# Decode order in the last network, splits of the last expert, and the end of the retention stage rearranged together

## The chip, the cores and the metric

One core of one Trainium2 chip runs the program. The time is device microseconds (us) of one execution of the whole program; lower is better. The engines are TensorE (PE, matrix products), VectorE (DVE), ScalarE (ACT), GpSimd (POOL) and SyncE (SP, which only issues DMAs here). Each works off its own instructions in the order in which the program wrote them, and waits at an instruction until what it needs is there.

## What is computed

Three networks in a row: a retention layer, a mixture of eight experts with one expert per token and limited places, and a network with a maximum of three products.

```python
def _attn_ref(q, k, v):                      # (4, 8, 576, 64) each
    scores = scale * np.matmul(q, k.transpose(0, 1, 3, 2))
    Dmat = np.where(rel >= 0, gamma[:, None, None] ** rel[None, :, :], 0.0)
    ret = scores * Dmat[None, :, :, :]
    return np.matmul(ret, v).astype(np.float32)

def _moe_ref(x, w_gate, w1, w2, capacity):   # x (2304, 512), E = 8, F = 1024
    logits = x @ w_gate
    expert_idx = np.argmax(logits, axis=1)
    ...                                      # probs: softmax; gate_w: its value at expert_idx
    for i in range(N):
        e = expert_idx[i]
        if counts[e] < capacity:
            disp[e, counts[e]] = x[i]; pos[i] = counts[e]; counts[e] += 1; keep[i] = True
    h = np.maximum(np.einsum('ecd,edf->ecf', disp, w1), 0.0)
    y = np.einsum('ecf,efd->ecd', h, w2)
    ...                                      # out[i] = gate_w[i] * y[expert_idx[i], pos[i]] where keep

def _moe2_ref(x, w1, w2, w3, w_out):         # 512 -> 768 -> 512
    h = np.maximum(np.maximum(x @ w1, x @ w2), x @ w3)
    return (h @ w_out).astype(np.float32)
```

Products are made in a precision close to float32: each operand is held as a high and a low part, and a product is three matmuls (high by high, high by low, low by high; L1095 to L1097, and their likes at L1135 and L1291).

## The kernel before

**Retention and gating (0 to 132 us).** The 2304 tokens go in 18 chunks of at most 128 rows (5 per batch element; the fifth has 64). A loop over `t` makes the scores of the next chunk (`scores`, `cut`), its outputs (`outputs`), and for earlier chunks the transposes (`transposes`, L487), the choice of expert (`gate1`, `position`, `gate2`), and the send of the scaled row into the DRAM table `xd`. Chunks 0 to 13 are gated in three groups (`group_choose`, `group_place`, `group_weigh`, `group_send`); a group is placed at the chunk two behind its last, and two of its rows of chunks are sent per chunk from then on. The last chunks (`NPATCH` = 3: 15, 16, 17) go to expert 0 another way: their rows don't come back out of `xd`. Expert 0's input is collected in the four PSUM tiles `fx`: `patch(u, c)` (L612) multiplies the rows of chunk u (`part`, high and low) by a selection matrix, and `turn(c)` (L620) adds, transposed, the rows that three indirect DMAs of POOL (`load_x(0)`, L170, r0 to r2) gathered from `xd`. `finish_part` makes the low part of `part` on DVE (L550) and sends the scaled `xg`. `seats` (L636) makes the tables of places. `first_x` splits `fx` into the high and low part that expert 0 reads.

**Experts (132 to 369 us).** For each expert, `mm1` has eight steps f (an output tile of 128 of the 1024 hidden columns, written as h by ACT, L1111, and its low part by DVE), and `mm2` four. Weights come as raw tiles of 512 KB (three buffers), and `next_split` makes the high part on ACT (L140) and the low part on DVE (L145) and then issues the next load on SP. A split stands behind each odd f and each step of `mm2`, and for expert 0 behind f = 2, 4 and 6 as well.

**Decode.** The last network's weights arrive as 64-bit numbers and are turned into float32 on the chip, in 24 pieces of 512 columns (`NDEC`): two ACT operations (`dec_act`, L1005 and L1006), four on DVE (`decode_top` L1020, L1023; `decode` L1031, L1034), two on POOL (L1037, L1038), and a write of POOL's queue to the DRAM table `wdec`. `NSOON` of them, 12, are decoded in the expert stage, at the steps that the table `per` names, and are loaded and split like other weights later. `per` has a tuple for each expert, of its 12 steps (eight f, then four of `mm2`).

**The pair (368.6 to 470.0 us).** The last network has six tiles of 384 tokens (i) and six hidden tiles (f). `up(i, f)` makes three products of 36 matmuls in all, into three of the six PSUM tiles; ACT copies the first (L1265, into m, or into a free part of y), DVE takes two maxima (L1266, L1267), ACT writes h (L1268) and DVE its low part (L1269). The first 12 steps, i = 0 and 1 in turn for each f, are the pair. In it the remaining 12 pieces are decoded. A late piece lies in a part of y, with two places in turn: `dec_act(n + 1)` waits until piece n - 1 has been written out of it. `take_unit` (L1063 on ACT, L1064 on DVE) makes the unit w out of a finished piece. How many pieces follow each step is the list `LATER`:

```python
LATER = [1, 1, 1, 2, 1, 1, 2, 1, 2]
        ...
                for _ in range(LATER[step] if step < len(LATER) else 0):
                    if n > NSOON:
                        take_unit(n - 1)
                    decode_top(n)
                    done[n] = decode(n)
                    n += 1
                    dec_act(n)
```

After the pair, `down` (L1291) and `up` for the other tiles run to 702.2 us.

## Time and profile before

| | us |
|---|---|
| median of three runs | 703.53 (703.26 to 704.21) |
| the profiled execution | 704.04 |
| its span | 702.2 |
| PE busy | 658.9 (94%) |
| DVE busy | 353.3 (50%) |
| ACT busy | 258.1 (37%) |
| POOL busy | 196.7 (28%) |

The span begins with the first instruction and ends with the last one; 1.84 us of the profiled execution's time lie outside it. All times of rows are counted from the start of the span. Busy shares are means over four stages that have different limits, so they are only a first look; which engine waits in a stage, and for whom, is read from the waits of PE, from its windows and from the chain of waits. The "granted clock" of a window is TensorE's clock as a share of 2.4 GHz; 0.50 is the lower of its two levels, 1.2 GHz.

### The profile page before, as it was taken

To read this page: it belongs to the slowest core of one execution; us is meant where nothing else is said; L and a number is where in the kernel's file an instruction comes from. 1 tells how busy PE (TensorE), PEld (TensorE's weight loads), DVE (VectorE), ACT (ScalarE), POOL (GpSimd) and SP (SyncE) were. 2 spreads that over 40 slices of the span, in tenths; PEclk is the share of its full clock that TensorE was granted. 3 is DMA by queue.
4 is the path that set the end of the run, shared out by engine and by line. 5 is a ranking of instruction groups with operands and counts; after the bars stand their busy time and mean duration, and the time that the engine had idled before them with its cause. 6 is when DMAs were issued, how large, how long until landed. Compare 5 with 4: busy or idle time off the path is not lost.

```text
span 702.2 us, 11814 instructions
## 1 busy us (share of the span) xinstructions
PE 658.9 (94%) x4631; PEld 623.2 (89%) x4631; DVE 353.3 (50%) x727; ACT 258.1 (37%) x478; POOL 196.7 (28%) x180
## 2 busy tenths in 40 slices
PE   8998997989999999999999957789999999999995
PEld 6887876989999999999999957788999999998994
DVE  3487686565757777776465646560032131131120
ACT  3344343255555556465454333331112121111111
POOL 1001122136555652677401354431100100101001
PEclk9999999599999999999999989789999999999998
DMA  8999932265786878767432333301100100000001
GB/s 279 326 265 291 356 96 61 94 177 188 221 196 203 237 218 245 212 218 210 134 135 68 117 102 116 109 30 46 46 0 1 46 1 15 31 1 31 15 1 47
DMA packets 42930, 91.01 MB, mean 130 GB/s; under 512 B 16778, under 2 KB 18702, under 8 KB 42872
## 3 DMA queue, kind: packets, MB, share of 16 engines
q1 hardware_dynamic: 25848, 64.73, 30.2%
q0 software_dynamic: 14624, 21.36, 9.7%
q10 hardware_dynamic: 2400, 4.14, 1.6%
q8 instruction: 38, 0.62, 0.4%
q14 instruction: 20, 0.16, 0.1%
HBM read 73.68 MB, written 16.47 MB: 128 GB/s over the span
## 4 chain that ended last, share of the span: by engine, by line
PE 73%; DMA 9%; ACT 5%; DVE 5%; issue 4%; POOL 3%; ACTq 1%; SPq 0%; POOLq 0%; DVEq 0%
PE b L1135 16%; PE u L1095 8%; PE u L1096 8%; PE u L1097 8%; PE a L1095 5%; PE a L1096 5%; PE a L1097 5%; PE d L1292 3%; PE d L1293 3%; PE d L1291 3%; DMA wdec<-y 3%; DMA kv<-in_kv_dram 2%; PE xps L487 2%; PE tp L968 1%; DMA xr<-xd,who 1%
## 5 line engine op out<-in xcount | busy, mean ns | idle before, releaser
L1095 PE MATMUL u<-ys,w 128*128 128x384 f32 x414 | 141.7, 342 | 18.9 <-ACT y L1265 8.2
L1096 PE MATMUL u<-ys,w 128*128 128x384 f32 x414 | 140.8, 340 | 0.0
L1097 PE MATMUL u<-ys,w 128*128 128x384 f32 x414 | 140.7, 340 | 0.0
L1135 PE MATMUL b<-h,w 128*128 128x336 f32 (+7 forms) x768 | 118.4, 308 | 3.3 <-ACT h L1111 2.7
L145 DVE TENSOR_TENSOR w<-raw,w 128x1024 fp32r<-128x1024 f32 x70 | 93.5, 1335 | 52.8 <-ACT w L140 45.3
L1135 PEld LDWEIGHTS b<-h,w 128*128 128x128 f32 x768 | 109.8, 190 | 4.4 <-ACT h L1111 3.3
L1095 PEld LDWEIGHTS u<-ys,w 128*128 128x128 f32 x414 | 79.8, 193 | 20.4 <-ACT y L1265 8.5
L1266 DVE TENSOR_TENSOR m<-u,m 128x384 f32<-128x384 f32 x30 | 16.7, 557 | 131.5 <-PE u L1097 115.9
L140 ACT ACTIVATE w<-raw 128x1024 fp32r<-128x1024 f32 x70 | 73.9, 1056 | 18.5 <-DMA raw<-in_weights_dram 17.0
L1096 PEld LDWEIGHTS u<-ys,w 128*128 128x128 f32 x414 | 79.9, 193 | 0.2
L1097 PEld LDWEIGHTS u<-ys,w 128*128 128x128 f32 x414 | 79.6, 192 | 0.2 <-DVE w L1064 0.2
L1095 PE MATMUL a<-xt,w 128*128 128x336 f32 (+7 forms) x256 | 78.5, 307 | 0.0
L1096 PE MATMUL a<-xt,w 128*128 128x336 f32 (+7 forms) x256 | 78.3, 306 | 0.0
L1097 PE MATMUL a<-xt,w 128*128 128x336 f32 (+7 forms) x256 | 78.2, 305 | 0.0
L1297 POOL DMA_INDIRECT out_dram<-o,perm_sb x18 | 17.4, 968 | 213.4 <-ACT o L1295 209.3
L1268 ACT ACTIVATE h<-m 128x384 fp32r<-128x384 f32 x28 | 14.7, 526 | 106.2 <-DVE m L1267 106.2
L1095 PEld LDWEIGHTS a<-xt,w 128*128 128x128 f32 x256 | 48.9, 191 | 0.9 <-issue 0.5
L1096 PEld LDWEIGHTS a<-xt,w 128*128 128x128 f32 x256 | 49.0, 191 | 0.0
L1097 PEld LDWEIGHTS a<-xt,w 128*128 128x128 f32 x256 | 48.9, 191 | 0.0
L170 POOL DMA_INDIRECT xr<-xd,who x24 | 37.3, 1554 | 35.3 <-DVE order_w L1156 21.9
L183 POOL DMA_INDIRECT who_d<-tok,slots_i x20 | 21.1, 1054 | 91.8 <-DMA who_d<-tok,slots_i 49.5
L1111 ACT ACTIVATE h<-a 128x336 fp32r<-128x336 f32 (+7 forms) x64 | 26.6, 423 | 33.6 <-PE a L1097 30.7
(216 smaller groups left out, 1025.8 us busy)
## 6 DMA issues: line engine op xcount, KB each, us to landing
raw<-in_weights_dram SPq DMA_DIRECT2D x64, 512.0 KB
kv<-in_kv_dram SPq DMA_DIRECT2D x16, 512.0 KB
qk<-in_qk_dram SPq DMA_DIRECT2D x15, 512.0 KB
y<-in_weights_dram SPq DMA_DIRECT2D x12, 512.0 KB
d<-in_weights_dram POOLq DMA_DIRECT2D x10, 512.0 KB
xd<-xg ACTq DMA_DIRECT2D x14, 256.0 KB
wdec<-mag POOLq DMA_DIRECT2D x12, 256.0 KB
raw<-wdec SPq DMA_DIRECT2D x6, 512.0 KB
```

Of the source, the lines that this page charges most:

```text
L140: act.activation(out=t[:, 0], in_=raws[w], func=AF.Copy)
L145: engine.tensor_tensor(out=t[:, 1], in0=raws.pop(w), in1=t[:, 0].bitcast(F32), op=ALU.subtract)
L170: pool.indirect_dma_start(out=xr[:n, r, :], out_offset=None, in_=xd[:, :], in_offset=bass.IndirectOffsetOnAxis(ap=who[:n, r, e : e + 1] if ...
L183: pool.indirect_dma_start(out=who_d[:, :], out_offset=bass.IndirectOffsetOnAxis(ap=slots_i[:L, t : t + 1], axis=0), in_=tok[:L, t : t + 1] ...
L1095: pe.matmul(ps, lhsT=wh, rhs=xh, start=first, stop=False)
L1096: pe.matmul(ps, lhsT=wh, rhs=xl, start=False, stop=False)
L1097: pe.matmul(ps, lhsT=wl, rhs=xh, start=False, stop=last)
L1111: act.activation(out=h[:, 0, :wide], in_=ps, func=AF.Relu)
L1135: pe.matmul(ps, lhsT=w[:, a, f * P : (f + 1) * P], rhs=hs[f][:, b, :wide], start=(i == 0), stop=(i == len(todo) - 1),)
L1291: pe.matmul(ps, lhsT=hh, rhs=wh, start=(f == 0), stop=False)
L1292: pe.matmul(ps, lhsT=hh, rhs=wl, start=False, stop=False)
L1293: pe.matmul(ps, lhsT=hl, rhs=wh, start=False, stop=(f == NFF - 1))
```

## The change

Four parts, all at once.

1. **Pair.** `NSOON` goes from 12 to 16, so 8 pieces stay for the pair, one for each of its first eight steps. The four more early ones: one in expert 5 (at place 5), two in expert 6 (5 and 8), one in expert 7 (2). The work on a piece is no longer written behind the step but inside `up`, by three callbacks: a finished piece's high part goes ahead of the maxima, the decode's four DVE operations stand between the maxima and the low part of h, and the finished piece's low part and the next `dec_act` follow behind it. 72 instead of 70 units are split; the last `next_split` stands behind the last `mm2`.
2. **Splits.** The extra splits at f = 2, 4, 6 go from expert 0 to expert 7.
3. **Groups.** The sends of groups 0 and 1 start one chunk later, and their `group_place` is moved into the middle of `outputs`; the last group's stays, now ahead of `cut(t + 1)`.
4. **End of retention.** `finish_part(16)` is done in the loop: ACT scales `xg` first, and POOL subtracts for the low part. `position(17)` no longer stands behind turns; then come `patch(16, c)`, the turns of r0 and r1 for all c, `seats(16)`, and in `first_x` for each c the turn of r2 with `patch(17, c)`; `seats(17)` and the count come after.

```diff
 NDEC = 2 * NFF * NPIECE
-NSOON = NDEC // 2
-LATER = [1, 1, 1, 2, 1, 1, 2, 1, 2]
+NSOON = 2 * NDEC // 3
...
                         )
+                    dve.tensor_tensor(out=acc[:L], in0=acc[:L], in1=oh[:L], op=ALU.add)
                     rows(t, xg, xps, g2)
...
                 part, xg, g2 = patch_t[t][0][0], xg_t.pop(t), g_t.pop(t)
-                dve.scalar_tensor_tensor(
-                    out=part[:L, 1], in0=xg[:L], scalar=g2[:L], in1=part[:L, 0].bitcast(F32),
-                    op0=ALU.mult, op1=ALU.subtract,
-                )
-                act.activation(out=xg[:L], in_=xg[:L], func=AF.Copy, scale=g2[:L])
+                if t == NCHUNK - 2:
+                    act.activation(out=xg[:L], in_=xg[:L], func=AF.Copy, scale=g2[:L])
+                    pool.tensor_tensor(out=part[:L, 1], in0=xg[:L], in1=part[:L, 0].bitcast(F32), op=ALU.subtract)
+                else:
+                    dve.scalar_tensor_tensor(
+                        out=part[:L, 1], in0=xg[:L], scalar=g2[:L], in1=part[:L, 0].bitcast(F32),
+                        op0=ALU.mult, op1=ALU.subtract,
+                    )
+                    act.activation(out=xg[:L], in_=xg[:L], func=AF.Copy, scale=g2[:L])
                 sp.dma_start(out=xd[1 + t0 : 1 + t0 + L, :], in_=xg[:L])
...
-            def turn(c):
-                for r, n in slots_of(0):
-                    pe.matmul(
-                        fx[c][:, r * RP : r * RP + n], lhsT=xr_t[0][:n, r, c * P : (c + 1) * P],
-                        rhs=ident[:n, :n], start=False, stop=False, skip_group_check=True,
-                    )
+            def turn(c, r, n):
+                pe.matmul(
+                    fx[c][:, r * RP : r * RP + n], lhsT=xr_t[0][:n, r, c * P : (c + 1) * P],
+                    rhs=ident[:n, :n], start=False, stop=False, skip_group_check=True,
+                )
             def first_x():
                 xt = xpool.tile([P, 2, NC, TILE2], F32R, tag="xt", name="xt0")[:, :, :, : WIDTH[0]]
                 for c in range(NC):
+                    turn(c, *slots_of(0)[-1])
                     patch(NCHUNK - 1, c)
                     split_x(xt, c, fx[c])
                 xt_t[0] = xt
...
                 for j in range(len(g)):
-                    sends.setdefault(g[-1] + 2 + j // 2, []).append((i, j))
+                    sends.setdefault(g[-1] + 2 + (i < len(GROUPS) - 1) + j // 2, []).append((i, j))
             for t in range(NCHUNK):
...
                     gate1(t - 1)
-                if t + 1 in sc_t:
+                early = t in placed and placed[t] == len(GROUPS) - 1
+                if t + 1 in sc_t and not early:
                     cut(t + 1)
...
                     update(t + 1)
-
-                if t in placed:
+                if early:
                     group_place(placed[t])
+                    cut(t + 1)
                 def place():
+                    if t in placed and not early:
+                        group_place(placed[t])
                     if ok(t - 1) and t - 1 not in GROUP_OF:
...
                     pick(t - 1)
-                    if t < NCHUNK - 1:
-                        finish_part(t - 1)
+                    finish_part(t - 1)
                 if ok(t - 1) and t - 1 not in GROUP_OF:
...
             seats(first)
-            seats(last - 1)
-            turn(0)
-            turn(1)
             position(last)
-            finish_part(last - 1)
             gate2(last)
             gate3(last)
-            for c in range(2, NC):
-                turn(c)
             for u in range(first + 1, last):
...
                     patch(u, c)
+            for r, n in slots_of(0)[:-1]:
+                for c in range(NC):
+                    turn(c, r, n)
+            seats(last - 1)
+            first_x()
             seats(last)
...
             dve.tensor_copy(out=cnt, in_=cnt_p)
-            first_x()
...
-        def take_unit(n):
+        def into_unit(n):
...
                 units[w] = home.tile([P, 2, 1024], F32R, tag="w", name=f"w{w}")
-            t = units[w]
-            act.activation(out=halves(t[:, 0, cols]), in_=mag, func=AF.Copy)
-            dve.tensor_tensor(
-                out=halves(t[:, 1, cols]), in0=mag, in1=halves(t[:, 0, cols]).bitcast(F32), op=ALU.subtract
-            )
+            hi, lo = (halves(units[w][:, k, cols]) for k in range(2))
+            act.activation(out=hi, in_=mag, func=AF.Copy)
+            return lambda: dve.tensor_tensor(out=lo, in0=mag, in1=hi.bitcast(F32), op=ALU.subtract)
         LAST = F // P + NC
-        per = [(8,), (2, 8), (2, 8), (2, 8), (2, 8), (2, 8), (2,), ()]
+        per = [(8,), (2, 8), (2, 8), (2, 8), (2, 8), (2, 5, 8), (2, 5, 8), (2,)]
         slots = [e * LAST + k for e in range(E) for k in per[e]]
...
                     units.pop(8 * e + f // 2)
-                if f % 2 or (e == 0 and f in (2, 4, 6)):
+                if f % 2 or (e == E - 1 and f in (2, 4, 6)):
                     if (e, f) != (0, 1):
...
         m2p = m2["pool"]
+        next_split()
         for c in range(NC):
...
-        def up(i, f, m, h):
+        def up(i, f, m, h, beside=(lambda: None,) * 3):
             wa, wb = units[8 * E + 2 * f], units[8 * E + 2 * f + 1]
...
             act.activation(out=m, in_=pss[0], func=AF.Copy)
+            beside[0]()
             dve.tensor_tensor(out=m, in0=pss[1], in1=m, op=ALU.max)
...
             act.activation(out=hi, in_=m, func=AF.Copy)
+            beside[1]()
             dve.tensor_tensor(out=lo, in0=m, in1=hi.bitcast(F32), op=ALU.subtract)
+            beside[2]()
             h2_t[i, f] = h
...
         early_h = m2p.tile([P, 2, NC, TILE2], F32R, tag="ys", name="early_h")
-        step, n = 0, NSOON
-        dec_act(n)
+
+        after = {}
+
+        def before_max(n):
+            if n in done:
+                after[n] = into_unit(n)
+
+        def behind_max(n):
+            if n < NDEC:
+                decode_top(n)
+                done[n] = decode(n)
+
+        def behind_h(n):
+            if n - 1 in after:
+                after.pop(n - 1)()
+            if n + 1 < NDEC:
+                dec_act(n + 1)
+
+        dec_act(NSOON)
+        n = NSOON
         for f in range(NFF):
             for i in range(2):
-                up(i, f, new_m(i, f), early_h[:, :, 2 * f + i] if f < 2 else new_h(i, f))
-                for _ in range(LATER[step] if step < len(LATER) else 0):
-                    if n > NSOON:
-                        take_unit(n - 1)
-                    decode_top(n)
-                    done[n] = decode(n)
-                    n += 1
-                    dec_act(n)
-                if step == len(LATER):
-                    take_unit(n - 1)
-                    assert n == NDEC
+                up(
+                    i, f, new_m(i, f), early_h[:, :, 2 * f + i] if f < 2 else new_h(i, f),
+                    (lambda: before_max(n - 1), lambda: behind_max(n), lambda: behind_h(n)),
+                )
+                n += 1
                 if (i, f) == (0, NFF - 1):
...
                         ysplit_part(2, c)
-                step += 1
         down(0)
```

How the order of the engines changes is shown at three places.

PE at the end of the retention stage, before (`fx_1654` to `fx_1657` are the four tiles c, `xr_1517` the gathered rows with r0 and r1 as x2, `po` is position(17)):

```order
L620 MATMUL fx_1655<-cst,xr_1517 128x118 x2
L620 MATMUL fx_1655<-cst,xr_1517 128x100
L493 LDWEIGHTS tri
L493 MATMUL po_1701<-oh_1682,tri 64x8
L499 LDWEIGHTS ones
L499 MATMUL po_1701<-acc,ones 64x8
L620 MATMUL fx_1656<-cst,xr_1517 128x118 x2
L620 MATMUL fx_1656<-cst,xr_1517 128x100
L620 MATMUL fx_1657<-cst,xr_1517 128x118 x2
L620 MATMUL fx_1657<-cst,xr_1517 128x100
L612 MATMUL fx_1654<-sel_1643,part_0_1644 128x336 x2
L612 MATMUL fx_1655<-sel_1643,part_0_1644 128x336 x2
```

After (tiles `fx_1657` to `fx_1660`):

```order
L492 LDWEIGHTS tri
L492 MATMUL po_1695<-oh_1685,tri 64x8
L498 LDWEIGHTS ones
L498 MATMUL po_1695<-acc,ones 64x8
L617 MATMUL fx_1657<-sel_1643,part_0_1644 128x336 x2
L617 MATMUL fx_1658<-sel_1643,part_0_1644 128x336 x2
L617 MATMUL fx_1659<-sel_1643,part_0_1644 128x336 x2
L617 MATMUL fx_1660<-sel_1643,part_0_1644 128x336 x2
L624 MATMUL fx_1657<-cst,xr_1517 128x118
L624 MATMUL fx_1658<-cst,xr_1517 128x118
L624 MATMUL fx_1659<-cst,xr_1517 128x118
L624 MATMUL fx_1660<-cst,xr_1517 128x118
```

Position(17) and the patches of chunk 16 moved ahead of all turns; r1 (four more rows of the same kind), three rows of `who_p` and then r2 in turn with the patches of chunk 17 follow.

DVE in the pair, step i = 1, f = 1, before (`y<-u` the maxima, `early_h` the low part of h, `w` a finished piece's low part, `y<-y` the decode):

```order
L1266 TENSOR_TENSOR y<-u_1_1_4746,y 128x2x192
L1267 TENSOR_TENSOR y<-u_1_2_4747,y 128x2x192
L1269 TENSOR_TENSOR early_h<-y,early_h 128x384
L1064 TENSOR_TENSOR w_4789<-y,w_4789 128x512
L1020 TENSOR_SCALAR y<-y 128x2x256
L1023 SCALAR_TENSOR_TENSOR y<-y 128x2x256
L1031 SCALAR_TENSOR_TENSOR y<-y 128x2x256
L1034 TENSOR_SCALAR y<-y 128x2x256
L1064 TENSOR_TENSOR w_4789<-y,w_4789 128x512
L1020 TENSOR_SCALAR y<-y 128x2x256
L1023 SCALAR_TENSOR_TENSOR y<-y 128x2x256
L1031 SCALAR_TENSOR_TENSOR y<-y 128x2x256
```

After:

```order
L1271 TENSOR_TENSOR y<-u_1_1_4808,y 128x2x192
L1272 TENSOR_TENSOR y<-u_1_2_4809,y 128x2x192
L1025 TENSOR_SCALAR y<-y 128x2x256
L1028 SCALAR_TENSOR_TENSOR y<-y 128x2x256
L1036 SCALAR_TENSOR_TENSOR y<-y 128x2x256
L1039 TENSOR_SCALAR y<-y 128x2x256
L1275 TENSOR_TENSOR early_h<-y,early_h 128x384
L1069 TENSOR_TENSOR w_4847<-y,w_4847 128x512
```

One decode in place of two, and it moved ahead of the low part of h; the second decode of this step is gone.

ACT in expert 7's first products, before (`h` the output of a step f, `w<-raw` a split):

```order
L1111 ACTIVATE h_2_4321<-a_2_4308 128x272
L1111 ACTIVATE h_3_4338<-a_3_4325 128x272
L140 ACTIVATE w_4341<-raw_4236 128x1024
L1111 ACTIVATE h_4_4359<-a_4_4346 128x272
L1111 ACTIVATE h_5_4376<-a_5_4363 128x272
L140 ACTIVATE w_4379<-raw_4268 128x1024
L1111 ACTIVATE h_6_4397<-a_6_4384 128x272
L1111 ACTIVATE h_7_4414<-a_7_4401 128x272
L140 ACTIVATE w_4417<-raw_4306 128x1024
```

After:

```order
L1114 ACTIVATE h_2_4353<-a_2_4340 128x272
L139 ACTIVATE w_4356<-raw_4262 128x1024
L1114 ACTIVATE h_3_4380<-a_3_4367 128x272
L139 ACTIVATE w_4383<-raw_4294 128x1024
L1114 ACTIVATE h_4_4401<-a_4_4388 128x272
L139 ACTIVATE w_4404<-raw_4332 128x1024
L1114 ACTIVATE h_5_4423<-a_5_4410 128x272
L139 ACTIVATE w_4426<-raw_4359 128x1024
L1114 ACTIVATE h_6_4444<-a_6_4431 128x272
L139 ACTIVATE w_4447<-raw_4386 128x1024
```

A split moved in behind f = 2, 4 and 6; in expert 0 these three splits went, and its steps look there as expert 7's did here.

## Rows read from the trace of the kernel before

**Rows 1.** Waits of PE over the span: total us, times, longest.

```profile
PE u L1095 <- ACT y L1265: 8.2, 1, 8.2
PE u L1095 <- ACT m L1265: 7.2, 1, 7.2
PE u L1095 <- ACT w L1063: 3.6, 1, 3.6
```

**Rows 2.** Windows of PE: length, busy (instructions), granted clock, DMA share, GB/s.

```profile
368.60:470.00 101.40, 82.51 (x434) 0.88 0.30 94
...
500.84:538.30 37.46, 37.46 (x217) 1.00 0.02 8
121.50:136.90 15.40, 15.40 (x60) 0.50 0.33 111
132.30:136.90 4.60, 4.60 (x17) 0.50 0.50 175
```

**Rows 3.** Chain of waits in the pair: start, us, what.

```profile
384.84 5.32 DMA wdec<-y
...
421.76 4.04 DMA wdec<-y
```

**Rows 4.** Groups of instructions in the pair, by shape: busy, mean ns, idle before.

```profile
L1037 POOL TENSOR_TENSOR y<-y 128x512 f32<-128x512 f32 x11 | 14.2, 1295 | 75.2 <-DVE y L1034 38.8 <-issue 26.8 <-ACT y L1265 5.5
...
L1031 DVE SCALAR_TENSOR_TENSOR y<-y 128x512 f32<-128x512 f32 x12 | 8.3, 692 | 0.4
...
L1005 ACT ACTIVATE y<-y 128x512 f32<-128x512 f32 x12 | 8.0, 669 | 40.2 <-DMA wdec<-y 31.9 <-DMA y<-in_weights_dram 3.9 <-DVE y L1034 3.1
L1064 DVE TENSOR_TENSOR w<-y,w 128x512 fp32r<-128x512 f32 x11 | 7.6, 692 | 11.1 <-ACT w L1063 11.1
...
L1034 DVE TENSOR_SCALAR y<-y 128x512 int32<-128x512 int32 x12 | 5.1, 427 | 0.4
...
L1266 DVE TENSOR_TENSOR m<-u,m 128x384 f32<-128x384 f32 x5 | 2.8, 558 | 15.6 <-ACT m L1265 15.6
```

**Rows 5.** Chain of waits in the retention stage.

```profile
59.52 12.43 DMA kv<-in_kv_dram
```

**Rows 6.** Timelines of ACT, then of PE, at the end of expert 0's first product.

```profile
151.62 1.06 ACT L140 ACTIVATE w<-raw 128x1024 fp32r<-128x1024 f32 x1 [5.43 <-DMA raw<-in_weights_dram]
...
149.22 2.00 PE L1135 MATMUL b<-h,w 128*128 128x336 f32 x12
153.07 0.58 PE L1135 MATMUL b<-h,w 128*128 128x336 f32 x2 [1.84 <-ACT h L1111]
154.51 3.11 PE L1135 MATMUL b<-h,w 128*128 128x336 f32 x10 [0.86 <-ACT h L1111]
```

**Rows 7.** Timelines of ACT in experts 5 and 7, then of DVE in expert 7.

```profile
298.58 1.06 ACT L140 ACTIVATE w<-raw 128x1024 fp32r<-128x1024 f32 x1 [2.56 <-DMA raw<-in_weights_dram]
...
350.74 0.40 ACT L1111 ACTIVATE h<-a 128x272 fp32r<-128x272 f32 x1 [1.11 <-PE a L1097]
...
352.24 0.40 ACT L1111 ACTIVATE h<-a 128x272 fp32r<-128x272 f32 x1 [0.15 <-PE a L1097]
...
352.12 1.23 DVE L145 TENSOR_TENSOR w<-raw,w 128x1024 fp32r<-128x1024 f32 x1 [0.51 <-ACT w L140]
```

**Rows 8.** End of retention: timelines of POOL, ACT, DVE, PE; line L1037's first use.

```profile
114.21 1.01 POOL L170 DMA_INDIRECT xr<-xd,who  x1 [0.30 <-issue]
...
116.25 0.72 ACT L529 ACTIVATE part<-xg,g 128x512 fp32r<-128x512 f32 x1 [1.29 <-DVE g L510]
...
124.27 0.16 DVE L507 TENSOR_TENSOR hit<-po,oh 64x8 f32<-64x8 f32 x1 [4.82 <-PE po L499]
...
121.49 2.46 PE L620 MATMUL fx<-cst,xr 118*128 118x118 f32 x10 [2.04 <-DMA xr<-xd,who]
...
L1037 POOLq MODIFY_POOL_CONFIG  x2: 50/50/50, 146.8 to 146.8; - x2
...
162.18 1.32 POOL L1037 TENSOR_TENSOR d<-d,top 128x512 f32<-128x512 f32 x1 [15.28 <-issue]
```

More of the change, by code (lines that the diff above doesn't have):

```diff
@@ L512, in gate2 @@
                 )
-                dve.tensor_tensor(out=acc[:L], in0=acc[:L], in1=oh[:L], op=ALU.add)
+                if t < NCHUNK - 1:
+                    dve.tensor_tensor(out=acc[:L], in0=acc[:L], in1=oh[:L], op=ALU.add)
                 pos_t[t], oh_t[t] = pos, oh
@@ L543, in gate2 @@
                         )
+                    dve.tensor_tensor(out=acc[:L], in0=acc[:L], in1=oh[:L], op=ALU.add)
                     rows(t, xg, xps, g2)
```

## The prediction

> **What bounds the kernel now.** I read the waits of TensorE (PE) first, since PE is busy for 659 of 702 us and a change can only win where PE waits or runs at its lower clock. Three waits of the up steps, 8.2, 7.2 and 3.6 us, are the only large ones; all stand at L1095, behind ScalarE (ACT), in the last network's pair [rows 1]. The windows of PE give that stage: 368.6 to 470.0 us, 101.4 us, at a mean granted clock of 0.88 [rows 2]. Six later up steps, undisturbed, take 37.46 us, so 6.24 us each; the twelve of the pair are worth 12 x 6.24 = 74.9 us. The excess is 101.4 - 74.9 = 26.5 us: 19.0 us of waits, and about 7.5 us that only the lower clock can hold, since PE's busy time of 82.5 us for the 74.9 of work is as much too long [rows 2]. The other places of lower clock are the end of the retention stage, 121.5 to 136.9 us at 0.50 (1.2 GHz), of which 4.6 us lie in expert 0's first products [rows 2], and expert 0's second product. The chain of waits in the pair runs from one landed write of a decoded piece (4.0 to 5.3 us) to the next [rows 3]. So what bounds the pair is the decode ring, not PE.
>
> **Pair (late pieces 12 to 8, one per up step, interleaved).** What a piece costs stands in the groups of the pair [rows 4]: two ACT operations of 0.67 us, DVE four operations (two of 0.69, two of 0.42), POOL two of 1.30. What an up step costs: ACT a copy and h, some 0.5 us each, DVE two maxima and the low half, 0.56 each; a finished piece adds a low half of 0.69 on DVE and some 0.62 on ACT. DVE then has 3 x 0.56 + 2.2 + 0.7 = 4.6 us of work in a step, 5.1 with gaps, and a step of PE lasts 6.24: it fits. Before, three steps held two pieces each, DVE's maxima stood behind whole decodes, and ACT's copy of the next step behind a wait for a write. What can still be late is the ring: piece n+1 takes the buffer of piece n-1, so over two steps (12.5 us) must fit: 1.35 (ACT) + 0.5 (copy) + 1.1 (maxima) + 2.2 (decode) + 2.6 (POOL) + 0.3 (issue) + 4.0 to 5.3 (landing) = 12.1 to 13.4 us, with gaps some 13 to 14. That loses about 0.4 us a step over seven steps, about 3 us, of which the six PSUM tiles (two steps) hide a part. The first piece also starts some 2.3 us later, because two more splits stand ahead of it (two of ACT at 1.06 [rows 7], DVE's halves beside them). I take a stall of 2 us, of 0.3 to 5.6: **24.5 us gained, 20.9 to 26.2**. The last four steps have no piece at all.
>
> **Expert 0 loses three splits.** In the trace a split on ACT (L140) waits 5.43 us for a raw tile, h6 and h7 stand behind it on ACT, and PE waits 1.84 and 0.86 us in the second product and then runs ten matmuls in 3.11 us [rows 6], 0.31 us each, against 0.17 in its twelve before; that is 1.35 us more. At most 1.84 + 0.86 + 1.35 = 4.05 us. With the wait gone, what is late next is expert 1's gather, issued where expert 0's h is done, and its transposes: up to 1.5 us. I take **3.0 gained, 0 to 4.05**.
>
> **Experts 5 to 7 take more.** Expert 5 waits already now for raw tiles on ACT: 2.56 us at 298.58 [rows 7]. A third piece there adds the 1.35 us on ACT and 2.2 on DVE of above and one more load and write of 256 KB; its 1.35 us and some of the traffic stand in front of raw tiles that are late already. I take 1.7 us lost there, and 0.7 in expert 6, whose one piece becomes three. Expert 7 gets one piece and the three splits, from f = 1 on one behind every f: from one h to the next are 1.50 us (350.74 to 352.24) [rows 7], and in that ACT has 0.40 + 1.05 to do and DVE 1.23 and the low half of h. Three raw tiles are in turn, so each must be split and loaded again in 3 x 1.50 = 4.5 us; 1.05 + 1.23 + a landing, whose nearest row is the 4.04 us of a write [rows 3], are 6.3. That is 1.8 us late per turn, and two turns fall between f = 2 and f = 7: at most 3.6 us at h7, as in expert 0 now. Some of it is covered by tiles loaded ahead; I take 2.6. **5 us lost, 0 to 9** (zero if the h are never what the second product waits for; nine if behind the waits of each of the three PE also runs 1.35 us longer at the lower clock, as in expert 0: 5 + 3 x 1.35).
>
> **End of the retention stage.** What is removed: the turns of expert 0's three gathers (r0 to r2) stand ahead of position(17) on PE, so DVE's hit(17) waits 4.82 us for it (at 124.27), and PE itself waits 2.04 us for a gather at 121.49 [rows 8], with the clock at 0.50 from then to 136.9 [rows 2]. After, position(17) goes ahead, patch(16) fills the wait for the gathers, and chunk 17's gates are done by then. What is added: patch(16) needs the low part that a POOL TENSOR_TENSOR now makes. POOL is free at 114.21 + 1.01 = 115.2, ACT's scaled xg is there at 116.25 + 0.72, plus 0.72 for the next, at 117.8; the operation takes 1.32 as L1037's, so the low part is there at max(115.3 + L, 117.8) + 1.35, with L the time of the MODIFY_POOL_CONFIG pair that the first POOL tensor_tensor carries ahead of it. This step is the unknown. Its two rows are 50 ns each, at 146.8, and the first operation behind them starts at 162.18, after 15.28 us without a visible cause [rows 8], right when its data came and at its usual length. So L lies between 0.1 and 15.3 us. I take 0.1, the length of the rows themselves, and keep both ends. With L up to 2.5: low part at 119.15, patches 16 to 120.3, turns r0 to 121.3, r1 (landed at 121.45) to 122.4, r2 and patch 17 to 124.6, seats 0.4: the first product starts at about 125.0 instead of 132.3, 7.3 us, and the 4.6 us of it at half clock save another 2.3. If the clock falls all the same, some 5 in all. I take **6.5 gained, -10 (L = 15.3) to +10**.
> For L = 5.2, a third of the way between the ends, the same steps give: low part at 121.85, PE without work from 118.8 for 3 us, longer than the 2.04 at which the clock is low now, so patches and turns run at 0.50 (2.3, 1.9, 1.9, 0.4 and 4.2 us, by the 2.46 us of ten turns [rows 8]), and the first product starts at about 132.5, as now: nothing gained.
> The Trainium skill says in the GPSIMD Engine Reference (section 2.1, Instruction dispatch) that the first call to a freshly loaded POOL kernel pays for a code load of some 6 us that no instruction of the profile shows. By that rule the part would lose some 0.8 us, and the whole would come to 682. The trace can't confirm it: 15.28 us of idle time would cover such a load, and the first call shows no surplus of its own (1.32 us against a mean of 1.30) [rows 4, 8].
>
> **Retention, groups 0 and 1 sent one chunk later.** The same number of instructions, moved by one chunk; that stretch (0 to 88 us) moves loads of which one alone took 12.43 us [rows 5], and it has no wait among the large ones of [rows 1]. A small wait for the group's choice may go, and others appear where the seven xg buffers are held longer. **0, -2 to +2.**
>
> **Sum.** 24.5 + 3.0 - 5.0 + 6.5 + 0 = 29.0 us. The profiled run took 704.04, 0.5 above the median, and gives 675.0; from the median of 703.53 it is 674.5.
>
> **The rivals.**
> B, the config pair decides: PE waits for the POOL instruction behind it, as worked out for L = 5.2, and the retention end gives 0 instead of +6.5, so 674.5 + 6.5 = **681** (677 to 686). For it: the two rows of 50 ns are followed by a long idle stretch, in which a cost of theirs is never seen. Against it: nothing in the trace shows one.
> C, the ring decides in the pair: if the writes land in 8 us instead of 4 to 5.3, two steps need 17 us against 12.5, 2.3 a step; over seven steps 16, of which PSUM hides some 4, so 12 instead of 2: 674.5 + 10 = **684.5** (681 to 690). For it: the order on ACT still waits for a landed write in every step; against it: in the densest stretch of now they land in 4.0 to 5.3.
> D, slower than before: transfers of the pair land like the kv load, 12.43 us [rows 5], loads and writes both. Two steps then need 21.5 us with gaps against 12.5, 4.5 a step and 31 over seven, less the 4 of PSUM, and the first piece's load and splits come 6 us later: the pair's excess is some 33 us against 26.5; with 3.0 gained and 5.0 lost in the experts and nothing at the retention end the sum is 703.5 + 6.5 - 3.0 + 5.0 = **712**. It decides from a landing of about 11 us; against it speaks that the DMA engines are busy for only 0.30 of the pair [rows 2].
> E, quicker than the forecast: expert 5 to 7 lose nothing and the full 10 us come at the retention end: 674.5 - 8.5 = **666**.
>
> **How the numbers follow.** Forecast 0.50 (668 to 679), B 0.28, C 0.14, D 0.04, E 0.04. The range goes from 666.5 to 687: it leaves out E's lower half, D and C's upper third, 0.02 + 0.04 + 0.05, and edges of the others, some 0.15 in all. A measurement of this kernel can tell 0.2% (1.4 us) from no change. Faster by more than that is all but D and a little of the meeting of C and losses: 0.95; within 0.2%: 0.01; slower: 0.04.
>
> **What would show it.** The pair's PE window close to 77 us at a clock of 1.00, without the waits of L1095 on ACT; one such wait of 7 us would mean C. The first products of expert 0 starting near 125.0 at full clock; starting near 133 with an idle POOL between its config rows and its TENSOR_TENSOR would mean B. No wait of PE on h in expert 0, and new ones of 1 to 3 us in expert 7, with the split's ACT row waiting for raw. The forecast is wrong as a whole if DVE, not the write, ends the steps of the pair.

## The result, and the profile after

The changed kernel takes 691.8 us (688.1 to 694.3), against 703.9 before: a ratio of 0.985, with an interval of 0.980 to 0.990. The forecast was 674.5, with a range of 666.5 to 687.0. Faster, then, but 12 us instead of 29, and outside the range. Its profiled execution took 694.25 us with a span of 692.4, 9.8 us less than the 702.2 of before. Single executions of one kernel lie up to some 7 us from their median here, so the total tells little of a part; each part is read from the stage in which it works. The profiled execution of one kernel below, tail_only, was a slow one (704.5 us, against a median of 699.1), so its stages stand in no table.

The span splits at six places of PE: the transposes of the last chunk (L487 before, L486 after), the first products of experts 0, 1 and 5, the first up step, the first `down`.

| stage, us | before | after | gained | forecast |
|---|---|---|---|---|
| start to the last transposes | 116.2 | 126.1 | -9.9 | 0 |
| from there to expert 0's first product | 16.1 | 12.4 | +3.7 | +6.5, with the clock |
| expert 0 | 37.5 | 32.7 | +4.8 | +3.0 |
| experts 1 to 4 | 119.3 | 120.3 | -1.0 | 0 |
| experts 5 to 7 | 79.5 | 87.6 | -8.1 | -5.0 |
| the pair | 101.4 | 80.9 | +20.5 | +24.5 |
| the rest | 232.2 | 232.3 | -0.1 | 0 |

Windows of PE in the changed kernel (length, busy with instructions, granted clock, DMA share, GB/s):

```profile
379.10:460.00 80.90, 76.32 (x434) 1.00 0.25 79
...
126.00:128.00 2.00, 2.00 (x9) 0.50 0.58 184
136.00:142.00 6.00, 4.75 (x19) 0.50 0.39 115
```

The first answers to the first of [rows 2]: the pair is 20.5 us shorter, and its clock is 1.00 instead of 0.88, but it is still 6 us above the 74.9 of its work. The other two are the end of the retention stage, where the clock falls to 0.50 twice, in other places than before.

Waits of PE over the span of the changed kernel (us in total, times, longest):

```profile
PE xps L486 <- ACT xg L384: 6.6, 2, 3.5
PE b L1138 <- ACT h L1114: 2.6, 2, 2.1
PE u L1098 <- ACT y L1269: 2.5, 3, 1.0
PE u L1098 <- ACT m L1269: 2.1, 2, 1.1
PE b L1138 <- DVE h L1115: 1.6, 2, 1.1
...
PE a L1098 <- DVE cnt L836: 1.2, 1, 1.2
```

The same wait of the transposes in the kernel before:

```profile
PE xps L487 <- ACT xg L385: 2.2, 3, 1.1
```

The waits of 8.2, 7.2 and 3.6 us [rows 1] are gone. The largest is now that of the transposes of the retention stage for ACT's copy into an xg buffer, 6.6 us against 2.2. Small waits of the up steps behind ACT are left, and new ones of the second product on ACT's h (expert 7) and on DVE's h (experts 5 and 6), and of expert 0's first product on the count.

### The profile page after: what moved, and what is told of

Read it like the earlier page. It is cut to its first block, busy times and chain, and to the rows that moved or that the text cites. A ratio compares the mean times of both kernels' runs of the same rounds, so it can differ in the third digit from the quotient of the medians.

```text
span 692.4 us, 11809 instructions
## 1 busy us (share of the span) xinstructions
PE 660.1 (95%) x4631; PEld 620.4 (90%) x4631; DVE 364.9 (53%) x724; ACT 256.1 (37%) x476; POOL 214.1 (31%) x185
## 4 chain that ended last, share of the span: by engine, by line
PE 65%; DVE 11%; DMA 10%; issue 5%; ACT 4%; POOL 4%; ACTq 0%; POOLq 0%; SPq 0%; DVEq 0%
PE b L1138 10%; PE u L1098 8%; PE u L1100 8%; PE u L1099 8%; PE d L1299 3%; PE d L1300 3%; PE d L1298 3%; PE a L1100 3%; PE a L1098 3%; PE a L1099 3%; DMA xd<-xg 2%; PE xps L486 2%; DMA who_d<-tok,slots_i 2%; DMA xr<-xd,who 2%; PE sc L265 2%
## 5 line engine op out<-in xcount | busy, mean ns | idle before, releaser
L1098 PE MATMUL u<-ys,w 128*128 128x384 f32 x414 | 138.9, 336 | 4.6 <-ACT y L1269 2.5
L1100 PE MATMUL u<-ys,w 128*128 128x384 f32 x414 | 138.4, 334 | 0.0
L1099 PE MATMUL u<-ys,w 128*128 128x384 f32 x414 | 138.4, 334 | 0.0
L144 DVE TENSOR_TENSOR w<-raw,w 128x1024 fp32r<-128x1024 f32 x72 | 100.9, 1402 | 44.9 <-ACT w L139 43.0
L1138 PE MATMUL b<-h,w 128*128 128x336 f32 (+7 forms) x768 | 119.7, 310 | 4.2 <-ACT h L1114 2.6
L139 ACT ACTIVATE w<-raw 128x1024 fp32r<-128x1024 f32 x72 | 75.9, 1055 | 23.2 <-DMA raw<-in_weights_dram 15.2
L1098 PEld LDWEIGHTS u<-ys,w 128*128 128x128 f32 x414 | 77.7, 188 | 6.4 <-ACT y L1269 3.5
L1099 PEld LDWEIGHTS u<-ys,w 128*128 128x128 f32 x414 | 77.7, 188 | 0.2
L1100 PEld LDWEIGHTS u<-ys,w 128*128 128x128 f32 x414 | 77.7, 188 | 0.0
L182 POOL DMA_INDIRECT who_d<-tok,slots_i x20 | 23.4, 1169 | 99.4 <-DMA who_d<-tok,slots_i 53.0
```

The lines of the kernel that those rows point to most:

```text
L139: act.activation(out=t[:, 0], in_=raws[w], func=AF.Copy)
L144: engine.tensor_tensor(out=t[:, 1], in0=raws.pop(w), in1=t[:, 0].bitcast(F32), op=ALU.subtract)
L182: pool.indirect_dma_start(out=who_d[:, :], out_offset=bass.IndirectOffsetOnAxis(ap=slots_i[:L, t : t + 1], axis=0), in_=tok[:L, t : t + 1] ...
L1098: pe.matmul(ps, lhsT=wh, rhs=xh, start=first, stop=False)
L1099: pe.matmul(ps, lhsT=wh, rhs=xl, start=False, stop=False)
L1100: pe.matmul(ps, lhsT=wl, rhs=xh, start=False, stop=last)
```

## The experiments

Stages of all profiled executions, in us (span of PE between the places named above):

| kernel | last transposes at | first product at | expert 0 | experts 5 and 6 | expert 7 | pair | span |
|---|---|---|---|---|---|---|---|
| before | 116.2 | 132.3 | 37.5 | 55.4 | 24.1 | 101.4 | 702.2 |
| after | 126.1 | 138.5 | 32.7 | 58.9 | 28.7 | 80.9 | 692.4 |
| sends_back | 119.9 | 132.2 | 32.8 | 62.5 | 28.8 | 81.1 | 689.5 |
| groups_only | 127.6 | 140.3 | 36.9 | 54.5 | 24.1 | 101.1 | 709.4 |
| pair_only | 119.7 | 134.9 | 37.7 | 59.3 | 24.1 | 81.2 | 689.1 |
| xg6 | 128.3 | 137.1 | 37.8 | 54.5 | 24.5 | 100.1 | 705.4 |
| lo_first | 119.4 | 131.1 | 33.5 | 59.4 | 27.4 | 78.7 | 681.6 |
| spread | 118.2 | 130.1 | 32.4 | 59.9 | 24.1 | 81.2 | 681.2 |
| all3 | 116.2 | 126.7 | 32.4 | 59.5 | 24.1 | 78.6 | 675.5 |
| no_write | 116.0 | 127.9 | 33.2 | 59.2 | 27.3 | 76.4 | 681.0 |
| dve_lo | 120.1 | 130.7 | 31.3 | 60.2 | 24.1 | 78.8 | 677.6 |
| best16 | 116.1 | 125.6 | 36.8 | 59.2 | 24.1 | 78.9 | 678.7 |
| best | 117.4 | 126.6 | 35.2 | 56.5 | 24.1 | 85.4 | 682.8 |

### The sends one chunk later: sends_back, groups_only, xg6

The theory came out of the trace of the changed kernel. Its ACT timeline in the retention stage, and the piece of the chain of waits that ends at the second row (start, us, what):

```profile
58.95 0.60 ACT L384 ACTIVATE xg<-xps 128x512 f32<-128x512 f32 x1 [5.53 <-DMA xd<-xg]
...
90.52 0.60 ACT L384 ACTIVATE xg<-xps 128x512 f32<-128x512 f32 x1 [6.89 <-DMA xd<-xg]
```

```profile
82.54 7.90 DMA xd<-xg
```

ACT copies a chunk into an xg buffer; the buffer is free when the row that it held has landed in `xd`. A send that starts one chunk later frees its buffer one chunk later, and here, where the DMA engines are busy for 0.96 of the time (82.5 to 90.5 us), the write itself takes 7.90 us. PE, whose next transposes need the PSUM tile that ACT is to empty, stands still. Behind the first wait PE also runs at a lower granted clock for a while, 0.54, where it was 1.00 before (window of PE):

```profile
60.00:70.00 10.00, 10.00 (x93) 0.54 0.87 294
```

Before, there is one such wait of ACT in this stage:

```profile
82.07 0.60 ACT L385 ACTIVATE xg<-xps 128x512 f32<-128x512 f32 x1 [3.04 <-DMA xd<-xg]
```

**sends_back**: the change without the later sends.

```diff
-                    sends.setdefault(g[-1] + 2 + (i < len(GROUPS) - 1) + j // 2, []).append((i, j))
+                    sends.setdefault(g[-1] + 2 + j // 2, []).append((i, j))
```

> The changed kernel, with the sends of groups 0 and 1 back at their old chunks; group_place stays inside outputs. Theory R (the seven xg buffers are held one chunk longer, so ACT's copy of a chunk waits for a landed write, 6.9 and 5.5 us in the changed kernel's trace): these waits go and expert 0's first product starts 8 to 10 us earlier, total 682 to 684. Rival P (the moved group_place on PE delays the chunks): the total stays at 690 to 694.

Measured: 687.5 us (684.5 to 691.2), ratio to before 0.975 (0.965 to 0.985). The last transposes come at 119.9 instead of 126.1, the first product at 132.2 instead of 138.5: 6.3 us from this one line, with `group_place` still moved. That is less than the 8 to 10 us that theory R expected, and the total is 3.5 us above its range; ACT's waits for a landed `xd` write fall from 13.3 us in all to 5.0, against 3.0 before, so they do not all go. The total of the profiled execution got less of it, since experts 5 and 6 took 62.5 us in it. Rival P does not explain the delay; what the moved `group_place` may still cost is within the scatter of the stage (below).

**groups_only**: before, with the third part of the change and nothing else (its lines stand in the diff above).

> The kernel before, with the change's third part alone (sends of groups 0 and 1 one chunk later, group_place inside outputs). Theory R: 8 to 10 us lost in the retention stage, total 711 to 714, with ACT waiting for xd<-xg. Rival: nothing lost by it alone (the delay in the changed kernel comes from another part), 702 to 705.

Measured: 712.5 us, ratio 1.014 (1.002 to 1.026). The last transposes come at 127.6, 11.4 us later than before, the first product at 140.3, 8.0 us later, and ACT shows the same two waits:

```profile
58.22 0.60 ACT L385 ACTIVATE xg<-xps 128x512 f32<-128x512 f32 x1 [5.71 <-DMA xd<-xg]
...
88.33 0.60 ACT L385 ACTIVATE xg<-xps 128x512 f32<-128x512 f32 x1 [7.94 <-DMA xd<-xg]
```

**xg6**: before, with one buffer less and no send moved (the line stands at three places).

```diff
-                xg_t[t] = wk.tile([P, DM], F32, tag="xg", name=f"xg{t}", bufs=7)
+                xg_t[t] = wk.tile([P, DM], F32, tag="xg", name=f"xg{t}", bufs=6)
```

> The kernel before, with six xg buffers instead of seven. Theory R (chunks wait for an xg buffer whose write to xd must have landed): with one buffer less the same wait appears without any later send, expert 0's first product starts 5 to 9 us later (137 to 141 us) and ACT L385 waits for xd<-xg by 5 us or more. Rival P (not the buffers): no change, 130 to 135 us.

Measured: 708.8 us, ratio 1.013 (1.005 to 1.022); the last transposes at 128.3, 12.1 us later than before, the first product at 137.1, at the lower edge of theory R's 137 to 141. The wait for a landed `xd` write appears without any later send:

```profile
56.35 0.60 ACT L385 ACTIVATE xg<-xps 128x512 f32<-128x512 f32 x1 [5.21 <-DMA xd<-xg]
...
84.54 0.60 ACT L385 ACTIVATE xg<-xps 128x512 f32<-128x512 f32 x1 [4.37 <-DMA xd<-xg]
```

The three together show the cause. In the ten profiled executions of the table with the old sends and seven buffers, the last transposes come between 116.0 and 120.1; with later sends or six buffers at 126.1, 127.6 and 128.3. So the time of one execution in this stage scatters by 4 us: pair_only, whose retention stage is that of before, has them at 119.7 against 116.2. The opposite edit, more than seven buffers, was not tried.

### The pair: pair_only, lo_first, no_write

**pair_only**: before, with the change's first part alone; the extra splits stay in expert 0.

> The kernel before, with the change's first part alone (16 pieces early, 8 late ones interleaved in the pair; 72 splits; the extra three splits stay in expert 0). Theory: the pair gains 20.5 us as in the changed kernel, experts 5 to 7 lose 3 to 4 us (of the 8 lost in the changed kernel the rest is due to the splits in expert 7), total 686 to 688. Rival: the loss in experts 5 to 7 is all due to the more pieces, 8 us, total 691 to 692.

Measured: 688.8 us (685.2 to 691.8), ratio 0.977 (0.966 to 0.988). The pair is 81.2 us, as in the whole change: it owes nothing to the other parts. Expert 7 keeps its 24.1 us although it has its piece, so the 4.6 us there are due to the splits; experts 5 and 6 lose 3.9.

What bounds the pair after the change is seen in its chain of waits, one step of it (start, us, what), and in what ended the idle time of `dec_act`'s first operation in the pair:

```profile
401.68 0.69 ACT y L1010
402.45 0.66 ACT y L1011
403.11 0.38 ACT m L1269
403.51 0.57 DVE m L1271
404.24 0.41 issue
404.65 0.43 DVE y L1025
405.10 0.70 DVE y L1028
405.83 0.70 DVE y L1036
406.60 0.30 issue
406.90 0.55 DVE early_h L1275
407.45 1.72 DVE w L1069
409.25 0.70 ACT y L1010
```

```profile
L1010 ACT ACTIVATE y<-y 128x512 f32<-128x512 f32 x8 | 5.4, 675 | 27.5 <-DVE w L1069 23.3 <-DMA y<-in_weights_dram 4.2
```

The step is 409.25 - 401.68 = 7.57 us, against 6.24 of PE; five such steps follow each other, up to 439.41, of 7.55 us in the mean. No transfer is in it. `dec_act(n + 1)` on ACT waits for the low part of piece n - 1 on DVE (L1069), which stands last in the step, because it still reads the buffer; the next copy of an up step (L1269) stands behind that `dec_act` on ACT; the maxima, the decode and h follow. So ACT and DVE work one after the other, not side by side. And L1069 takes 1.80 us, against 0.69 before [rows 4], as it runs beside POOL's two operations, which are longer too (1.49 and 1.63 instead of 1.30). Timelines of DVE and POOL there:

```profile
407.37 1.80 DVE L1069 TENSOR_TENSOR w<-y,w 128x512 fp32r<-128x512 f32 x1
```

```profile
407.13 1.49 POOL L1042 TENSOR_TENSOR y<-y 128x512 f32<-128x512 f32 x1 [3.29 <-issue]
408.70 1.63 POOL L1043 TENSOR_TENSOR y<-y 128x512 f32<-128x512 f32 x1
```

**lo_first**: the changed kernel without its third part, and the low part of piece n - 1 ahead of the decode.

```diff
         def behind_max(n):
+            if n - 1 in after:
+                after.pop(n - 1)()
             if n < NDEC:
...
         def behind_h(n):
-            if n - 1 in after:
-                after.pop(n - 1)()
```

> The changed kernel without its third part (groups as before), and in the pair the low part of a finished piece goes ahead of the decode on DVE instead of behind the low part of h, so that the next dec_act need not wait for the whole step. Theory S (the steps of the pair end in one chain of ACT and DVE, 7.55 us, in which the finished piece's low part stands last and takes 1.80 us instead of 0.69 since POOL's multiply runs beside it): the pair falls from 81 to 76 to 78 us. Rival W (the write of the piece before last ends the step): the pair stays at 80 to 82.

Measured: 682.9 us (681.8 to 683.4), ratio 0.973 (0.966 to 0.980). Its pair, the groups of the two instructions in it, and a piece of its chain:

```profile
370.70:449.30 78.60, 76.11 (x434) 1.00 0.26 85
```

```profile
L1007 ACT ACTIVATE y<-y 128x512 f32<-128x512 f32 x8 | 5.4, 670 | 24.3 <-DMA wdec<-y 17.9 <-DMA y<-in_weights_dram 4.0 <-DVE y L1036 2.4
...
L1066 DVE TENSOR_TENSOR w<-y,w 128x512 fp32r<-128x512 f32 x8 | 5.5, 686 | 4.4 <-ACT w L1065 4.2
```

```profile
409.33 6.07 DMA wdec<-y
```

The pair falls by 2.3 us to 78.7, a little above what theory S expected. L1066, the same low part, is back at 0.69 us, and what ACT's L1007 waits for is now the write (17.9 us of 24.3).

**no_write**: lo_first, and the eight late pieces are not written to `wdec`; only the path for tokens over an expert's width, which these inputs do not take, would read them.

```diff
-            out_ = wdec[rows, cols]
-            pool.dma_start(out=out_ if n < NSOON else halves(out_), in_=mag)
+            if n < NSOON:
+                pool.dma_start(out=wdec[rows, cols], in_=mag)
```

> lo_first without the write of the eight late pieces to the table wdec (left out here; only the path for tokens over an expert's width would read it). Theory W2 (with the low part ahead of the decode, the landing of the write of the piece before last, 4.1 to 6.1 us, is what ends the steps): the pair falls from 78.7 to 75 to 76.5 us, at 74.9 PE never waits. Rival (DVE or ACT itself ends the steps): it stays above 78.

Measured: the pair takes 76.4 us (window below), as theory W2 expected, so the write's landing is worth 2.2 us.

```profile
367.10:443.60 76.50, 75.54 (x435) 1.00 0.18 60
```

The total, 685.2 us, is not lower than that of lo_first: some 5 us come in behind the last `down`, where POOL's drain at the program's end takes 5.54 us instead of 0.72. Why it does is open.

### The splits of the last expert: spread, and what was put together

Expert 7 in the changed kernel: timeline of ACT, then of PE.

```profile
360.57 1.06 ACT L139 ACTIVATE w<-raw 128x1024 fp32r<-128x1024 f32 x1 [1.37 <-DMA raw<-in_weights_dram]
...
365.82 1.06 ACT L139 ACTIVATE w<-raw 128x1024 fp32r<-128x1024 f32 x1 [1.32 <-DMA raw<-wdec]
```

```profile
367.22 1.14 PE L1138 MATMUL b<-h,w 128*128 128x272 f32 x6 [2.15 <-ACT h L1114]
```

Each split waits for its raw tile, by 1.2 to 1.4 us, h stands behind it, and PE stands still for 2.15 us in the second product. A window of PE right behind that wait shows the lower clock:

```profile
367.90:371.30 3.40, 3.40 (x17) 0.51 0.88 264
```

**spread**: the changed kernel without its third part, and the three splits one each in experts 1 to 3.

```diff
-                if f % 2 or (e == E - 1 and f in (2, 4, 6)):
+                if f % 2 or (e, f) in ((1, 4), (2, 4), (3, 4)):
```

> The changed kernel without its third part, and with the three extra splits one each in experts 1, 2 and 3 (f = 4) instead of all in expert 7. Theory E (the three raw buffers can't be turned round once per f): expert 7 falls from 28.7 to 24 to 25.5 us, expert 0 stays at 32.7, experts 1 to 3 within 1 us of now. Rival (expert 7 is late because of its piece, not of the splits): expert 7 stays at 28 or more.

Measured: 683.0 us, ratio 0.972 (0.963 to 0.981). PE in expert 7, from its first product to the first up step:

```profile
343.60:367.70 24.10, 24.10 (x195) 1.00 0.60 193
```

Busy throughout, in 24.1 us as before, with its piece. Expert 0 keeps what it won; expert 3 takes 30.8 instead of 29.3 and expert 2 0.4 more. Theory E holds; the loss in expert 3 is 1.5 us against before, 0.9 against the changed kernel.

**all3**: lo_first, spread, and `seats(17)` and the count ahead of the last patches.

> Both edits of the two kernels above at once, and the places of chunk 17 and the count ahead of the last patches again. Theory: the sum of the parts, 4.5 us (expert 7), 4 us (pair) and 1 to 2 us (no wait for the count before expert 0), so 9 to 11 us below the changed kernel without its third part, some 675 to 678.

Measured: 679.6 us (677.1 to 684.2), ratio to before 0.971 (0.963 to 0.979): 1.4 points below the changed kernel's ratio, and none of the others is faster beyond the intervals. That is above the 675 to 678 expected; the parts by stage are 4.8 us (expert 7), 2.5 (pair) and 1.8 (first product), against sends_back. The first product follows 10.5 us after the last transposes, without a wait for the count.

**best16** and **best** tried to go on from there.

```diff
-                    turn(c, *slots_of(0)[-1])
                     patch(NCHUNK - 1, c)
...
-            for r, n in slots_of(0)[:-1]:
+            for r, n in slots_of(0):
...
-                if f % 2 or (e, f) in ((1, 4), (2, 4), (3, 4)):
+                if f % 2 or (e, f) in ((1, 2), (1, 6), (2, 4)):
```

> all3 with the turns of all three gathers ahead of the patches of chunk 17 and the extra splits at f = 2 and 6 of expert 1 and f = 4 of expert 2. Theory: turning r2 in one row instead of between patches saves 0.3 us for each of the four tiles, and experts 3 and 4 lose nothing, 1 to 3 us below all3: 675 to 678.

Measured: 680.2 us, ratio 0.973 (0.967 to 0.979), not better than all3. The first product does come 1.0 us sooner (9.5 us behind the last transposes), and expert 0's first products run at a granted clock of 1.00, where all3's ran at 0.50 for 2 us; so PE is at expert 1's transposes by 144.2 instead of 146.8, too early for expert 1's gather, which the prediction named as late next, and expert 0 takes 36.8 us. Largest wait of PE there:

```profile
PE tp L969 <- DMA xr<-xd,who: 2.8, 2, 2.4
```

For best, `NSOON` is 14 and the two pieces at place 5 of experts 5 and 6 are left to the pair.

> best16 with 14 early pieces instead of 16 (the ones at place 5 of experts 5 and 6 left out), so ten late ones. Theory N (the third pieces of experts 5 and 6 cost 2 us each): experts 5 and 6 fall from 59.5 to 56 us in sum, and the pair with two more pieces rises by less than 2: 673 to 677. Rival (their loss is not due to the pieces, since they took 59.2 in tail_only without them): no gain there, the pair 1 to 3 us longer, 677 to 681.

Measured: 683.7 us, ratio 0.976 (0.969 to 0.982). Experts 5 and 6 do fall, to 56.5 us, but the pair rises by 6.4, not by 2. The largest wait of PE in it:

```profile
PE u L1094 <- ACT w L1064: 4.3, 1, 4.3
```

An up step now stands and waits for a piece that is decoded too late. In the table, experts 5 and 6 take 54.5 to 56.5 us with two and one piece, or two each, and 58.9 to 62.5 with three each: the pieces cost some 4 us by that. But in tail_only's execution they took 59.2 us without a third piece, so the figure is not shown to be theirs alone.

### The end of the retention stage: tail_only, dve_lo

**tail_only**: before, with the change's fourth part alone.

> The kernel before, with the change's fourth part alone (end of the retention stage). By the prediction's step with a short config pair: 6.5 us gained, total 697. By the changed kernel's trace (16.1 us from the last transposes to expert 0's first product become 12.4): 3.7 us gained and 0 to 1 of clock, total 699 to 700. By the rival with a long config pair: 703.5.

Measured: 699.1 us, ratio 0.991 (0.985 to 0.996), so 2.9 to 10.3 us gained. That rules out a gain of nothing, the rival with a long config pair, and holds both the 6.5 of the prediction and the 3.7 of the changed kernel's trace.

**dve_lo**: all3, with the low part of chunk 16 on DVE.

```diff
-                if t == NCHUNK - 2:
+                if t < 0:
```

> all3 with the low part of chunk 16 on DVE as before, still in the loop, so that the config pair of POOL goes back behind the gathers. Theory (the pair costs at most 2.5 us and is hidden): expert 0's first product within 1.5 us of all3's, counted from the last transposes (10.5 us). Rival B of the prediction (PE waits for the operation behind the config pair): 3 to 6 us less.

Measured: 10.7 us from the last transposes to the first product, against 10.5 in all3; 682.9 us, ratio 0.978 (0.972 to 0.984). So POOL's operation with its config pair is not seen to cost PE anything, though the last transposes of this execution came 3.8 us later than all3's, which by itself can shorten this stretch (xg6: 8.8 us). The trace of the changed kernel has the bound itself (instructions of line L553, then ACT's timeline):

```profile
L553 POOLq MODIFY_POOL_CONFIG  x2: 33/36/38, 124.9 to 125.0; - x2
...
L553 POOL TENSOR_TENSOR part<-xg,part x1: 1266/1266/1266, 127.5 to 127.5; 128x512 fp32r<-128x512 f32 x1
```

```profile
126.71 0.72 ACT L552 ACTIVATE xg<-xg,g 128x512 f32<-128x512 f32 x1
```

The config pair stands at 124.9 to 125.0. ACT's xg ends at 126.71 + 0.72 = 127.43, and the first TENSOR_TENSOR starts at 127.52: it waited for its data and for nothing else. In the eight other kernels that have this operation it starts 0.08 to 0.09 us behind the end of ACT's xg, too. The pair takes 2.5 us at most, and the patches that read the low part start at 129.60, 0.8 us after it is there.

## Why the prediction was wrong

**Groups 0 and 1 sent later, 0 (-2 to +2): the step that failed most.** Measured -9.9 at the last transposes, in a stage that scatters by 4 us; at the first product, the edit alone cost 8.0 and its removal gave 6.3, so some 6 to 8 of the 19 us that are missing. The prediction counted the instructions, which are the same, and saw that "others appear where the seven xg buffers are held longer", but set no price on it. The price could have been read: the stage is full of transfers, a kv load took 12.43 us in it [rows 5], and a send moved by one chunk keeps two buffers of seven one chunk longer. A moved send is a moved release, and its price can be estimated as one landing for each time round, less the slack that the ring shows: 3.04 us of wait before say that there was none. Two groups were moved, and ACT's waits for landed writes rose by 10.3 us, from 3.0 to 13.3.

**Pair, 24.5 (20.9 to 26.2): the mechanism right, the limit another.** Measured 20.5. The step that failed is "DVE then has 3 x 0.56 + 2.2 + 0.7 = 4.6 us of work in a step, 5.1 with gaps, and a step of PE lasts 6.24: it fits". Work of one engine was added up, but ACT's and DVE's operations wait for each other in turn through one buffer, and their sum is 7.57 us. The prediction named the sign itself: it is wrong as a whole "if DVE, not the write, ends the steps of the pair". Of the 6.0 us over 74.9 the order of one low part is worth 2.3 and the write 2.2, by lo_first and no_write; the ring over the landing, which the prediction took for the limit, becomes it only when that chain is opened. What is left is 1.5. The other reason for the long chain, 1.80 us for an operation of 0.69, stood in no row of [rows 4], where that operation never ran beside POOL's; but the trace of before has it in the splits of the expert stage (last section).

**Experts 5 to 7, -5 (0 to -9).** Measured -8.1, inside the bounds: 4.6 in expert 7, where 2.6 was taken: the wait itself is 2.15, and the clock that falls behind it, as in expert 0 before, stood only in that term's bound; and 3.5 in 5 and 6, where 2.4 was. In expert 7 the mechanism, raw tiles that can't be turned round once per f, is as forecast, and spread confirms it. In 5 and 6 it is not what PE's waits show: PE waits there for DVE, 1.6 us for h and 1.3 for the transposed rows, and DVE's splits beside POOL's work on a piece take up to 2.88 us instead of 1.23. No run tests that part by itself.

**Expert 0, +3.0 (0 to 4.05).** Measured +4.8, 0.7 above the bound: the whole stall of [rows 6] went, and the lower clock at its start lasts some 4 us instead of 4.6; the rest is open. So the move of the splits gave 4.8 and took 4.6: it moved a stall from one expert to another. Experts 1 to 3, which have more time for each f, take the three for about 2.

**End of retention, +6.5 (-10 to +10).** Measured +3.7 by the stage. Where the last transposes are late, this stage is shorter even without the fourth part: 12.7 us in groups_only and 8.8 in xg6, against 16.1. With the sends at their old chunks the changed order took 11.6 to 12.3 (sends_back, lo_first, spread, no_write), the old one 15.1 and 16.1 (pair_only, before): 3 to 4.5 us gained, so the 3.7 stands. Rival B, with its chance of 0.28, is refuted: no config pair holds PE. The Trainium skill's rule for the first call (GPSIMD Engine Reference, section 2.1) isn't borne out for this operation, and the measurement decides. What was mis-sized is the rest. PE's timeline there:

```profile
129.60 1.50 PE L617 MATMUL fx<-sel,part 128*128 128x336 f32 x8
130.94 1.98 PE L624 MATMUL fx<-cst,xr 118*128 118x118 f32 x16
...
132.89 0.44 PE L624 MATMUL fx<-cst,xr 100*128 100x100 f32 x2
133.27 0.57 PE L617 MATMUL fx<-sel,part 64*128 64x336 f32 x2
...
136.03 0.92 PE L617 MATMUL fx<-sel,part 64*128 64x336 f32 x2
...
138.54 0.62 PE L1098 MATMUL a<-xt,w 128*128 128x336 f32 x1 [1.25 <-DVE cnt L836]
```

The patches and the sixteen rows of r0 and r1 take 3.3 us together (129.60 to 132.89), as forecast. But r2 in turn with the patches of chunk 17 takes some 0.9 us for each c and 4.1 us in all (132.89 to 136.95), where 2.2 were set; the first product waits 1.25 us for the count, which the change put behind the patches; and the clock falls again, at 126 and at 136. In no_write, whose last transposes came at 116.0, the first product came at 127.9, not at 125.0: 4.4 us gained where 7.3 were forecast, and nothing of clock: the first 4 us of expert 0 ran at 0.50 there as before.

Rivals C and D did not come about: the writes land in about 4 to 6 us (chains of before and lo_first), and nothing in the pair is late by 12. The upper end of the range follows rivals B and C, which change one term each of the likeliest sum, and does not ask what comes when several miss on the same side: of five terms only expert 0's came out better than forecast.

## What to carry to other kernels

Of a transfer that is sent later, ask which buffer it frees, how many there are, and whether anything waits for one already; count landings, not instructions. A duration read from a trace holds for the neighbours that the operation had there; ask what runs beside it after the change. Where two engines hand a buffer back and forth, add their operations up in series along the wait, since each fits into the step by itself. A stall that is moved to another stage is gained only if that stage has time for each turn of the ring that it must refill.

## What the runs showed of the hardware

A DVE operation with two inputs in SBUF took 1.80 us beside two operations of POOL (seven times, L1069), and 0.68 to 0.69 alone, in the same kernel too; POOL's took 1.49 and 1.63 instead of 1.30. The Trainium skill says in the GPSIMD Engine Reference (section 1, Specifications) that POOL shares its SBUF interfaces with DVE and that DVE instructions with two SBUF inputs contend; the traces agree, and give the size for DVE here, a factor of 2.6. POOL's first operation took 1.49 in lo_first too, where it overlaps only the end of DVE's low part of h.

The factor is no constant. DVE's L1069 ends 0.55 us behind the end of POOL's first operation, and POOL's second 1.16 us behind the end of L1069, as if each had waited for the other's end. A split of the kernel before, 1.23 us alone [rows 7], shows the same (timelines of DVE and POOL):

```profile
211.06 2.22 DVE L145 TENSOR_TENSOR w<-raw,w 128x1024 fp32r<-128x1024 f32 x1
```

```profile
210.89 1.30 POOL L1037 TENSOR_TENSOR d<-d,top 128x512 f32<-128x512 f32 x1 [5.17 <-DVE top L1034]
212.27 2.18 POOL L1038 TENSOR_TENSOR mag<-mag,d 128x512 f32<-128x512 f32 x1
```

It ends 1.1 us behind the end of POOL's first operation, and POOL's second 1.2 us behind its end. So what such an operation pays depends on how much of the other's is still to run.

The write of 256 KB from an xg buffer took 7.90 us in the retention stage and a write of the same size 4.0 to 6.1 us in the pair.
